# A two-layer network after linear attention: seven-product multiplication of the second product taken one level further from the third strip on

## The chip, the cores and the metric

The kernel runs on one NeuronCore of a Trainium2 chip. The time is the device time in microseconds of one execution. Everything is fp32. TensorE (PE) multiplies from SBUF into PSUM banks; VectorE (DVE) and ScalarE (ACT) read PSUM and SBUF; GpSimd (POOL) works in SBUF; SyncE (SP) issues the transfers. Each engine runs its instructions in the order in which they were written.

## What is computed

```python
# q, k, v: (8, 8, 576, 64); w_in: (512, 2048); w_out: (2048, 512), given as 64-bit floats
kv = np.einsum('bhsd,bhse->bhde', k, v)
out = np.einsum('bhsd,bhde->bhse', q, kv)
rms = np.sqrt(np.mean(out * out, axis=-1, keepdims=True) + 1e-06)
x = (out / rms * g_norm)                 # then (B, H, S, D) -> (4608, 512)
h = x @ w_in
r = np.maximum(h, 0.0)
y = (r * r) @ w_out                      # (4608, 512)
```

## The kernel before

The 4608 rows of x are 36 tiles of 128, worked off in nine strips of four tiles (512 rows). A strip has a first product, x @ w_in with the squared ReLU, and a second one with w_out. While a strip is multiplied, the attention work for the next one is done in small slices between the steps.

**Products.** Apart from strip 0's first product (`up_first`, L579, 512-column matmuls), each product is one level of a seven-product scheme of Strassen's kind: the operands are cut in halves both ways, seven products of halves with prepared sums are formed instead of eight, and the results are put together. `up` (L597) does it for each of four groups g of the 2048 hidden features: seven products p in `ORDER` (L536), each of 2 x 2 matmuls with 256 columns. `down` (L631) does it for the second product: seven products, each two steps i of eight matmuls with 256 columns. `product` (L548) issues them all, on L551. The banks are A (two of them), B and C: `open_bank` (L542) opens one for p = 1, 5, 2, later products accumulate into them. `combine` (L556) takes the results out: ACT copies `snap` of p = 1, 6, 5, and one addition for each of 2, 7, 3, on DVE; p = 4 is copied by ACT.

**Operand sums.** The hidden quarters 11, 12, 21, 22 and a fifth tile 1 for a sum are `gt` tiles of 128 x 2048 from `g_pool` (five). `sums_g` (L575) makes two differences or sums per group in the first product; `down` makes two more over whole quarters (L643, L645). `sums_x` (L469) makes four sums of x, as a slice, when the strip's four tiles are there. w_in lies in SBUF with its sums (`sums_in`, L235). w_out's seven blocks lie in DRAM (`w_out`, L164) and are streamed, 1 MB per product, into three slots (`stream`, L625): each is asked for when a product has ended.

**Attention slices** (L479 to L511): `transposed_query` and `key_value` for each pair of heads of a batch, then per tile `query` (products, root mean square, scaling) and, from the third batch on, `squares_x`, which turns the tile by way of DRAM, and `scale_x` (L459), which multiplies by g_norm on ACT. `attend` at L699 spreads a strip's slices over 85% of its steps' weight. `key_value` asks for the next pair's k, v, q (`load_next`) into three slots each; the store of the output, eight transfers for one `o_sb` tile, is issued on SP too (L656), as are all loads.

**Strip 0** also converts w_in and w_out from 64-bit floats: `convert_on_act` on ACT, `conversion` on DVE, `sums_out` (L246) for w_out's sums. The `raw` slots of this work are given back at L688, and the pools opened there take their place.

## Time and profile before

| | |
|---|---|
| median of 3 runs | 987.95 us (987.73 to 988.01) |
| profiled execution | 989.48 us, of it 987.7 us span from the first to the last instruction |
| mean granted TensorE clock | 0.994 |
| strip 0's first product begins | 38.6 us |
| strip 0's second product begins | 101.6 us |
| strip 1's first product begins | 158.5 us |
| last strip's second product | 932.5 to 980.7 us |
| DMA | 139.79 MB, mean 142 GB/s |

The span is what the trace covers; the execution's own time has a little around it. An engine's busy share is an average over stages with different limits. Matmuls are pipelined: the duration in a row (379 ns for 256 columns) is longer than the distance from one to the next. A source-level fp32 matmul shows as two instructions.

### The profile page before, as it was taken

To read this page: it belongs to the slowest core of one execution; us is meant where nothing else is said; L and a number is where in the kernel's file an instruction comes from. 1 tells how busy PE (TensorE), PEld (TensorE's weight loads), DVE (VectorE), ACT (ScalarE), POOL (GpSimd) and SP (SyncE) were. 2 spreads that over 40 slices of the span, in tenths; PEclk is the share of its full clock that TensorE was granted. 3 is DMA by queue.
4 is the path that set the end of the run, shared out by engine and by line. 5 is a ranking of instruction groups with operands and counts; after the bars stand their busy time and mean duration, and the time that the engine had idled before them with its cause. 6 is when DMAs were issued, how large, how long until landed. Compare 5 with 4: busy or idle time off the path is not lost.

```text
span 987.7 us, 12864 instructions
## 1 busy us (share of the span) xinstructions
PE 956.9 (97%) x4968; PEld 810.8 (82%) x4968; DVE 457.3 (46%) x826; ACT 244.7 (25%) x510; POOL 1.7 (0%) x7
## 2 busy tenths in 40 slices
PE   3799999999999999999999999999999999999997
PEld 3444888888888888888888888888888888888886
DVE  3899872463255424462356335343545155214320
ACT  3698311221122102211222122111321022002200
POOL 0000000000000000000000000000000000000000
PEclk9799999999999999999999999999999999999999
DMA  8689775425633463446344642475114610450041
GB/s 251 214 268 322 259 213 194 96 70 192 213 74 88 160 199 103 94 135 204 111 97 114 201 149 62 125 188 186 43 33 155 207 43 22 160 193 10 1 155 58
DMA packets 150108, 139.79 MB, mean 142 GB/s; under 512 B 84128, under 2 KB 130720, under 8 KB 142368
## 3 DMA queue, kind: packets, MB, share of 16 engines
q1 hardware_dynamic: 149888, 138.98, 46.2%
q8 instruction: 39, 0.64, 0.3%
q14 instruction: 21, 0.17, 0.1%
q10 hardware_dynamic: 160, 0.00, 0.0%
HBM read 115.08 MB, written 23.86 MB: 141 GB/s over the span
## 4 chain that ended last, share of the span: by engine, by line
PE 88%; DVE 6%; DMA 2%; ACT 2%; issue 1%; SPq 1%; DVEq 0%; ACTq 0%
PE ps_A L551 47%; PE ps_B L551 24%; PE ps_C L551 12%; PE x_ps L362 2%; PE kv_ps L333 2%; DVE w_c L208 1%; DVE wt L228 1%; DMA raw<-in_moe_w_out_dram 1%; DVE w_c L202 1%; DMA raw<-in_moe_w_in_dram 1%; DVE w_in L211 1%; DMA q_rest<-in_q_dram 1%; ACT w_c L190 0%; ACT raw L193 0%; DVE wt L211 0%
## 5 line engine op out<-in xcount | busy, mean ns | idle before, releaser
L551 PE MATMUL ps_A<-w_blk,gt 128*128 128x256 f32 x1120 | 249.0, 379 | 0.7 <-ACT snap L561 0.7
L551 PEld LDWEIGHTS ps_A<-w_blk,gt 128*128 128x128 f32 x1120 | 211.7, 190 | 29.6 <-ACT snap L561 1.1
L551 PE MATMUL ps_A<-x_t,w_in 128*128 128x256 f32 x768 | 182.6, 381 | 0.7 <-DVE gt L610 0.7
L551 PEld LDWEIGHTS ps_A<-x_t,w_in 128*128 128x128 f32 x768 | 144.8, 190 | 20.9 <-DVE gt L610 1.1
L551 PE MATMUL ps_B<-w_blk,gt 128*128 128x256 f32 x544 | 121.0, 379 | 0.0
L551 PEld LDWEIGHTS ps_B<-w_blk,gt 128*128 128x128 f32 x544 | 103.0, 190 | 13.8
L561 ACT COPY snap<-ps_A 128x512 f32<-128x512 f32 x82 | 47.9, 585 | 187.2 <-PE ps_A L551 187.2
L228 DVE TENSOR_TENSOR gt<-gt 128x512 f32<-128x512 f32 (+1 forms) x54 | 66.2, 1225 | 41.9 <-PE ps_A L551 23.1
L610 DVE TENSOR_TENSOR gt<-ps_C,snap 128x512 f32<-128x512 f32 x32 | 22.1, 692 | 128.3 <-PE ps_C L551 128.3
L610 DVE TENSOR_TENSOR gt<-ps_A,snap 128x512 f32<-128x512 f32 x32 | 22.1, 692 | 102.5 <-PE ps_A L551 102.3
L611 DVE SCALAR_TENSOR_TENSOR gt<-gt 128x512 f32<-128x512 f32 x96 | 66.5, 692 | 3.3
L551 PE MATMUL ps_A<-xT,w_in 128*128 128x256 f32 x256 | 61.0, 381 | 0.0
L551 PE MATMUL ps_B<-xT,w_in 128*128 128x256 f32 x256 | 61.0, 381 | 0.0
L551 PE MATMUL ps_C<-xT,w_in 128*128 128x256 f32 x256 | 60.6, 379 | 0.0
L551 PE MATMUL ps_B<-x_t,w_in 128*128 128x256 f32 x256 | 60.5, 379 | 0.0
L370 DVE TENSOR_REDUCE ms<-sq 128x8 f32<-128x512 f32 x36 | 24.6, 684 | 75.2 <-ACT sq L368 75.1
L551 PE MATMUL ps_C<-w_blk,gt 128*128 128x256 f32 x256 | 57.5, 380 | 0.0
L551 PEld LDWEIGHTS ps_C<-xT,w_in 128*128 128x128 f32 x256 | 48.6, 190 | 6.7 <-issue 0.2
L551 PEld LDWEIGHTS ps_A<-xT,w_in 128*128 128x128 f32 x256 | 48.2, 190 | 6.7
L551 PEld LDWEIGHTS ps_B<-xT,w_in 128*128 128x128 f32 x256 | 48.2, 190 | 6.6
L551 PEld LDWEIGHTS ps_B<-x_t,w_in 128*128 128x128 f32 x256 | 48.3, 190 | 6.4
L551 PEld LDWEIGHTS ps_C<-w_blk,gt 128*128 128x128 f32 x256 | 48.2, 190 | 6.6 <-issue 0.2
(90 smaller groups left out, 769.1 us busy)
## 6 DMA issues: line engine op xcount, KB each, us to landing
w_blk<-w_out SPq DMA_DIRECT2D x60, 1024.0 KB, 5.1
k<-in_k_dram SPq DMA_DIRECT2D x32, 256.0 KB, 3.1
v<-in_v_dram SPq DMA_DIRECT2D x32, 256.0 KB, 3.4
raw<-in_moe_w_in_dram SPq DMA_DIRECT2D x16, 512.0 KB, 6.4
raw<-in_moe_w_out_dram SPq DMA_DIRECT2D x16, 512.0 KB, 5.2
x_d<-x_q SPq DMA_DIRECT2D x27, 256.0 KB, 2.4
xT<-x_d SPq DMA_DIRECT2D x108, 64.0 KB, 2.0
q<-in_q_dram SPq DMA_DIRECT2D x96, 64.0 KB, 3.1
```

The lines of the kernel that those rows point to most:

```text
L202: yield nc.vector.tensor_scalar(out=c, in0=c, scalar1=LEAST, scalar2=MOST, op0=ALU.max, op1=ALU.min)
L208: yield nc.vector.scalar_tensor_tensor(out=ci, in0=high, scalar=-(2**30), in1=ci, op0=ALU.bitwise_and, op1=ALU.bitwise_or)
L211: yield nc.vector.tensor_tensor(out=dest.bitcast(I32), in0=ci, in1=r, op=ALU.add)
L228: eng.tensor_tensor(out=out, in0=a, in1=b, op=ALU.subtract)
L333: nc.tensor.matmul(ps[ts(h, D)], lhsT=a, rhs=w, start=c == 0, stop=c == C)
L362: nc.tensor.matmul(o, lhsT=qT[b, p][:, c_b, :], rhs=kvd[b, p], start=True, stop=True)
L370: nc.vector.reduce_sum(out=ms, in_=by_head(sq), axis=AX.X)
L551: nc.tensor.matmul(bank[BANK[p]][:, i, :], lhsT=lhsT(k), rhs=rhs(k), start=p in (1, 5, 2) and i == 0 and k == 0, stop=k == n - 1, skip_gro ...
L561: nc.scalar.copy(snap[p], b)
L610: nc.vector.tensor_tensor(out=o, in0=b, in1=a, op=ALU.add)
L611: nc.vector.scalar_tensor_tensor(out=o, in0=o, scalar=0.0, in1=o, op0=ALU.max, op1=ALU.mult)
```

## The change

Strips 0 and 1 (`DEEP = 2`) keep their second product. From strip 2 on each of its seven products is cut once more by the same scheme: 49 small products, each four matmuls with 128 columns. A level-1 product is two steps: the leaves 1, 2 and 4, whose left operands are plain blocks of a quarter, then 5, 6, 7 and 3, whose left operands are sums that `leaf_sums` makes on DVE one product ahead. Each level-1 product uses two PSUM banks, turn about on A+A and C+B; `together` takes the previous product's result out, with a copy on ACT and four additions on DVE, and adds the finished partial results into the output tiles. The sums over whole quarters (formerly `sums_g` and two differences) are made in the first and third product, two of them on GpSimd. The order of the seven is 4, 1, 2, 6, 5, 7, 3.

The right operands need W_out's sums of the second level: strip 1 makes them on DVE (`deep_sums`) and writes them to DRAM (`w_deep`). From strip 2 on a level-1 product streams two tiles, three blocks (0.75 MB) from `w_out` and four (1 MB) from `w_deep`, into four slots; `stream(2)` is called at a product's end, for the product after the next. `w_out` is laid out in column blocks of 128 for this and written in pieces of 512 bytes.

Along with it: g_norm is multiplied into w_in once (`sums_in`) instead of into x (`scale_x` is gone; strip 0's x keeps it); attention is spread over 42% of a strip's weight instead of 85%; `sums_x` is called at fixed steps; `g_pool` has four tiles instead of five, the fifth quarter being four small tiles (`g_s1`) in strips 0 and 1; strip 0's `sums_g` are all made at the start of its second product; q, k and v have two slots instead of three, pairs 2 and 3 of the first batch lie in `g_pool` slots, and two `load_next` calls of strip 0 are gone, one being added in `key_value`; `snap`, `o_sb` and the partial results share six slots (`c_pool`), the sums of x and of the quarters eight (`sum_pool`).

```diff
...
+    DEEP = 2
...
-    qkv_pool = ctx.enter_context(tc.tile_pool(name="qkv", bufs=3))
+    qkv_pool = ctx.enter_context(tc.tile_pool(name="qkv", bufs=2))
...
-    g_pool = ctx.enter_context(tc.tile_pool(name="g", bufs=5))
+    g_pool = ctx.enter_context(tc.tile_pool(name="g", bufs=4))
...
-    osb_pool = ctx.enter_context(tc.tile_pool(name="osb", bufs=2))
...
-    w_out = dram.tile([7, P, FQ, DH], FP32, name="w_out")
+    w_out = dram.tile([7, P, 2, FQ, P], FP32, name="w_out")
+    w_deep = dram.tile([7, P, 4, FQ // 2, P], FP32, name="w_deep")
...
     def sums_in(g):
+        nc.scalar.activation(w_in[:, :, g, 0:4], w_in[:, :, g, 0:4], AF.Copy, scale=g_col)
...
-            nc.sync.dma_start(out=w_out[3:7, :, j, :].rearrange("b p e -> p b e"), in_=x)
+            for e in range(2):
+                nc.sync.dma_start(out=w_out[3:7, :, e, j].rearrange("b p e -> p b e"), in_=x[:, :, ts(e, P)])
...
         if b < 2:
-            if b == 1 and p == 0:
+            if b == 1 and p < 2:
...
-        nc.scalar.activation(
-            x[:, ts(i, 4)].rearrange("p a q t -> p q a t"), ps.rearrange("p q (a t) -> p q a t", a=4),
-            AF.Copy, scale=g_col,
-        )
+        nc.scalar.copy(x[:, ts(i, 4)].rearrange("p a q t -> p q a t"), ps.rearrange("p q (a t) -> p q a t", a=4))
...
-    def scale_x(n):
-        s, i = divmod(n, NT)
-        o = xt[s][:, ts(i, 4)]
-        nc.scalar.activation(o, o, AF.Copy, scale=g_col)
...
-            xc_pool.tile([P, TH // SQ, KH, SQ], FP32, name=f"x_t{i}", tag=f"x_t{i}") for i in range(4)
+            sum_pool.tile([P, TH // SQ, KH, SQ], FP32, name=f"x_t{i}", tag="sum") for i in range(4)
...
-        for i in range(len(ns) + 2):
+        for i in range(len(ns) + 1):
...
-            done = ns[i - 1] if b < X_ON_PE and 0 < i <= len(ns) else ns[i - 2] if b >= X_ON_PE and i > 1 else None
-            if done is not None:
-                if b >= X_ON_PE:
-                    slices.append((scale_x, (done,)))
-                if done % NT == NT - 1:
-                    if done // NT:
-                        slices.append((sums_x, (done // NT,)))
-                    ready[done // NT] = len(slices)
+            if i > 0 and ns[i - 1] % NT == NT - 1:
+                ready[ns[i - 1] // NT] = len(slices)
...
    def quarters(s, g):
-        if (s, 1) not in gq:
-            for q in (11, 12, 21, 22, 1):
+        if (s, 11) not in gq:
+            for q in (11, 12, 21, 22):
...
-        return {q: gq[s, q][:, 2 * g : 2 * g + 2, :] for q in (11, 12, 21, 22, 1)}
-    def sums_g(dest):
-        nc.vector.tensor_tensor(out=dest[1], in0=dest[12], in1=dest[22], op=ALU.add)
+        return {q: gq[s, q][:, 2 * g : 2 * g + 2, :] for q in (11, 12, 21, 22)}
+    def sums_g(s, g):
+        dest = quarters(s, g)
+        s1 = gq[s, 1, g] = sum_pool.tile([P, 2, TH], FP32, name="g_s1", tag="sum")
+        nc.vector.tensor_tensor(out=s1, in0=dest[12], in1=dest[22], op=ALU.add)
...
-        if g > 0 and fh == 1 and i == 0:
-            sums_g(quarters(0, g - 1))
...
-                if q == 12:
-                    sums_g(dest)
+                if q == 12 and s < DEEP:
+                    sums_g(s, g)
...
-    w_blk[0, 1], w_blk[0, 2], w_blk[0, 5] = w_first
-    to_stream = iter([(s, p) for s in range(N_STRIP) for p in ORDER if (s, p) not in w_blk])
-    def stream():
-        u = next(to_stream, None)
-        if u is not None:
-            w_blk[u] = stream_pool.tile([P, FQ, DH], FP32, name="w_blk", tag="w_blk")
-            nc.sync.dma_start(out=w_blk[u], in_=w_out[B_OUT[u[1]]])
+    for p, t in zip((1, 2, 5), w_first):
+        w_blk[0, p] = t.rearrange("p f (h e) -> p h f e", h=2)
+    DEEP_ORDER = (4, 1, 2, 6, 5, 7, 3)
+    to_stream = [(s, p) for s in range(DEEP) for p in ORDER if (s, p) not in w_blk]
+    to_stream += [(s, p, n) for s in range(DEEP, N_STRIP) for p in DEEP_ORDER for n in range(2)]
+    to_stream = iter(to_stream)
+    def stream(n=1):
+        for _, u in zip(range(n), to_stream):
+            s, p = u[:2]
+            t = stream_pool.tile([P, 4, FQ // 2, P], FP32, name="w_blk", tag="w_blk")
+            if s < DEEP:
+                w_blk[u] = t.rearrange("p (h a) f e -> p h (a f) e", h=2)
+                nc.sync.dma_start(out=w_blk[u], in_=w_out[B_OUT[p]])
+            elif u[2] == 0:
+                nc.sync.dma_start(
+                    out=t[:, 1:4], in_=w_out[B_OUT[p]].rearrange("p h (a f) e -> p (h a) f e", a=2)[:, 1:4]
+                )
+                w_blk[s, p, 3], w_blk[s, p, 1], w_blk[s, p, 2] = (t[:, i] for i in range(1, 4))
+            else:
+                nc.sync.dma_start(out=t, in_=w_deep[B_OUT[p]])
+                w_blk[s, p, 5], w_blk[s, p, 6], w_blk[s, p, 7], w_blk[s, p, 4] = (t[:, i] for i in range(4))
+    def out_tile():
+        return c_pool.tile([P, 2, DH], FP32, name="o_sb", tag="c")
+    def send(s, th, eh, o):
+        for t in range(2):
+            for part, rows in out_rows(NT * s + 2 * th + t):
+                nc.sync.dma_start(out=rows[:, ts(eh, DH)], in_=o[part, t, :])
...
-        a = gq[s, {1: 11, 2: 21, 6: 11, 5: 1, 7: 12, 3: 21, 4: 22}[p]]
+        a = {1: 11, 2: 21, 6: 11, 7: 12, 3: 21, 4: 22}.get(p)
...
-        product(p, i, lambda fc: a[:, fc, ts(i, P)], lambda fc: w[:, fc, :], FQ)
+        product(
+            p, i,
+            lambda fc: (gq[s, 1, fc // 2][:, fc % 2] if p == 5 else gq[s, a][:, fc])[:, ts(i, P)],
+            lambda fc: w[:, :, fc], FQ,
+        )
         if i == 0:
+            if s == DEEP - 1:
+                deep_sums(p, w)
...
-        if s > 0 or p not in (1, 2, 5):
+        if s == 0 and p in (6, 7, 3) or s == DEEP - 1 and p not in (3, 4):
...
+        if s == DEEP - 1:
+            nc.sync.dma_start(out=w_deep[B_OUT[p]], in_=deep.pop(p))
         if p == 1:
-            minus(nc.vector, gq[s, 11], gq[s, 1], gq[s, 11])
+            for g in range(NG):
+                x = gq[s, 11][:, ts(g, 2)]
+                minus(nc.vector, x, gq[s, 1, g], x)
...
             def f(b, a=None):
-                o = osb_pool.tile([P, 2, DH], FP32, name="o_sb", tag="o_sb")
+                o = out_tile()
...
-                for t in range(2):
-                    for part, rows in out_rows(NT * s + 2 * th + t):
-                        nc.sync.dma_start(out=rows[:, ts(eh, DH)], in_=o[part, t, :])
+                send(s, th, eh, o)
...
+    deep = {}
+    def deep_sums(p, w):
+        t = deep[p] = stream_pool.tile([P, 4, FQ // 2, P], FP32, name="w_t", tag="w_blk")
+        b11, b12, b21, b22 = (w[:, e, ts(f, FQ // 2)] for f in range(2) for e in (1, 0))
+        minus(nc.vector, t[:, 0], b12, b11)
+        minus(nc.vector, t[:, 1], b22, t[:, 0])
+        minus(nc.vector, t[:, 2], b22, b12)
+        minus(nc.vector, t[:, 3], b21, t[:, 1])
+    A_G = {4: 22, 1: 11, 2: 21, 6: 11, 5: 22, 7: 12, 3: 21}
+    leaf, chain, part = {}, {}, {}
+    def leaf_sums(s, p):
+        a = gq[s, A_G[p]]
+        a11, a12, a21, a22 = (a[:, ts(f, FQ // 2), ts(t, P)] for t in range(2) for f in range(2))
+        s1, s2, s3, s4 = (sum_pool.tile([P, FQ // 2, P], FP32, name=f"g_s{i}", tag="sum") for i in range(4))
+        leaf[p] = {1: a11, 2: a12, 3: s4, 4: a22, 5: s1, 6: s2, 7: s3}
+        nc.vector.tensor_tensor(out=s1, in0=a21, in1=a22, op=ALU.add)
+        minus(nc.vector, s2, s1, a11)
+        minus(nc.vector, s3, a11, a21)
+        minus(nc.vector, s4, a12, s2)
+    PLACE = {1: (0, 0), 2: (0, 1), 6: (0, 2), 5: (1, 0), 7: (1, 1), 3: (1, 2), 4: (1, 3)}
+    def small_products(s, p, js):
+        c = "B" if p in (4, 2, 5, 3) else "A"
+        if js[0] == 1 and p not in (6, 7, 3):
+            chain[c] = [
+                fpsum.tile([P, 4, P], FP32, name=f"ps_{c}", tag=t, bufs=2 if t == "A" else 1)
+                for t in ("AA" if c == "A" else "CB")
+            ]
+        for j in js:
+            x, i = PLACE[j]
+            a, w = leaf[p][j], w_blk.pop((s, p, j))
+            for f in range(FQ // 2):
+                nc.tensor.matmul(
+                    chain[c][x][:, i, :], lhsT=a[:, f, :], rhs=w[:, f, :],
+                    start=p not in (6, 7, 3) and j in (1, 4) and f == 0, stop=f == FQ // 2 - 1, skip_group_check=True,
+                )
+    def together(p):
+        x, y = chain["B" if p in (4, 2, 5, 3) else "A"]
+        o = part[p] = out_tile()
+        q = o.rearrange("p t (h e) -> p (t h) e", h=2)
+        one = lambda t: t.to_broadcast([P, 2, P])
+        add = lambda out, a, b: nc.vector.tensor_tensor(out=out, in0=a, in1=b, op=ALU.add)
+        nc.scalar.copy(q[:, 3], x[:, 0])
+        add(q[:, 1:3], one(q[:, 3:4]), x[:, 1:3])
+        add(q[:, 0:4:3], one(q[:, 2:3]), y[:, 0:2])
+        add(q[:, 2], q[:, 3], y[:, 0])
+        add(q[:, 0:4:3], q[:, 0:4:3], y[:, 2:4])
+        for a, th, eh in {2: [(1, 0, 0)], 7: [(4, 1, 0), (5, 1, 1)], 3: [(6, 0, 1)]}.get(p, []):
+            add(part[a], part[a], o)
+            send(s, th, eh, part[a])
+    def down_deep(s, k, js):
+        p = DEEP_ORDER[k]
+        small_products(s, p, js)
+        before = DEEP_ORDER[k - 1] if k else None
+        after = DEEP_ORDER[k + 1] if k < 6 else None
+        g = lambda q: gq[s, q]
+        if js[0] == 1:
+            if k:
+                together(before)
+            if k == 0:
+                leaf_sums(s, after)
+                nc.vector.tensor_tensor(out=g(22), in0=g(12), in1=g(22), op=ALU.add)
+                minus(nc.gpsimd, g(12), g(11), g(12))
+            if k == 2:
+                minus(nc.vector, g(11), g(22), g(11))
+                minus(nc.gpsimd, g(21), g(21), g(11))
+            if 0 < k < 6:
+                leaf_sums(s, after)
+            if k == 6 and s + 1 < N_STRIP:
+                sums_x(s + 1)
+        else:
+            stream(2)
+            if k == 6:
+                together(p)
...
-        steps += [(2, down, (s, p, i)) for p in (ORDER if s else (1, 2, 5, 6, 7, 3, 4)) for i in range(2)]
+        if s < DEEP:
+            steps += [(2, down, (s, p, i)) for p in (ORDER if s else (1, 2, 5, 6, 7, 3, 4)) for i in range(2)]
+        else:
+            steps += [(2, down_deep, (s, k, js)) for k in range(7) for js in ((1, 2, 4), (5, 6, 7, 3))]
...
-                if i in (2, 4, 6):
+                if i in (2, 4):
...
-                xc_pool = ctx.enter_context(tc.tile_pool(name="xc", bufs=1, reuse_waits="tile"))
-                snap_pool = ctx.enter_context(tc.tile_pool(name="snap", bufs=1, reuse_waits="tile"))
-                stream_pool = ctx.enter_context(tc.tile_pool(name="stream", bufs=3, reuse_waits="tile"))
-                for _ in range(3):
-                    stream()
+                sum_pool = ctx.enter_context(tc.tile_pool(name="sum", bufs=8, reuse_waits="tile"))
+                c_pool = ctx.enter_context(tc.tile_pool(name="c", bufs=6, reuse_waits="tile"))
+                stream_pool = ctx.enter_context(tc.tile_pool(name="stream", bufs=4, reuse_waits="tile"))
+                stream(3)
+                for g in range(NG):
+                    sums_g(0, g)
...
-                    nc.sync.dma_start(out=w_out[b], in_=t)
+                    for e in range(2):
+                        nc.sync.dma_start(out=w_out[b, :, e], in_=t[:, :, ts(e, P)])
...
             if s:
-                attend(ready[s] + int((goal - ready[s]) * min(done / (0.85 * total), 1)))
+                attend(ready[s] + int((goal - ready[s]) * min(done / (0.42 * total), 1)))
+                if s >= DEEP and i == n_up - 3:
+                    leaf_sums(s, 4)
+                if s == DEEP - 1 and i == len(steps) - 1:
+                    sums_x(s + 1)
+                    stream(4)
...
-            if i == n_up:
-                sums_g(quarters(0, NG - 1))
...
             if i == n_up + 6:
-                load_next()
...
-                for g in range(NG):
-                    sums_in(g)
+            if i - n_up in (6, 8, 10, 12):
+                sums_in((i - n_up - 6) // 2)
+            if i == n_up + 9:
+                sums_x(1)
...
```

## Prediction

> **What bounds the kernel now.** I read the page first: busy shares and the chain of waits. Then the busy time by stage, the groups by shape, the timeline around one attention product, and the DMA issues.
>
> ```profile
> span 987.7 us, 12864 instructions
> ...
> PE 956.9 (97%) x4968; PEld 810.8 (82%) x4968; DVE 457.3 (46%) x826; ACT 244.7 (25%) x510; POOL 1.7 (0%) x7
> ...
> PE 88%; DVE 6%; DMA 2%; ACT 2%; issue 1%; SPq 1%; DVEq 0%; ACTq 0%
> ```
>
> TensorE (PE) is busy nearly throughout and is 88% of the chain. Where it is not the bound shows by stage (stretch, length, then busy time and instructions of PE, weight load, DVE, ACT, POOL, clock, DMA share, GB/s):
>
> ```profile
> 38.60:101.60 63.00, 63.00 (x230) 29.42 (x229) 61.22 (x137) 56.58 (x129) 0.00 (x0) 0.96 0.88 275
> 101.60:158.50 56.90, 55.59 (x291) 48.61 (x289) 37.52 (x76) 9.42 (x22) 0.00 (x0) 1.00 0.80 258
> 158.50:213.80 55.30, 54.61 (x326) 47.01 (x326) 27.18 (x48) 14.90 (x32) 0.00 (x0) 1.00 0.36 89
> 836.00:884.00 48.00, 48.00 (x225) 42.24 (x224) 10.85 (x12) 4.84 (x8) 0.00 (x0) 1.00 0.46 159
> ```
>
> The first two are strip 0's first and second product, the third strip 1's first, the last strip 7's second. From strip 1 on PE has no gap worth the name; strip 7's second product is 224 instructions in 48 us with DVE idle three quarters of the time. So PE instructions taken out there come off the span one for one, until DVE, a bank or a stream is late. Only strip 0 is also tight on DVE (61.2 of 63.0).
>
> The price of a PE instruction is its pace, not its duration, since they are pipelined:
>
> ```profile
> 480.02 1.89 PE L551 MATMUL ps_A<-x_t,w_in 128*128 128x256 f32 x8
> 640.53 1.08 PEld L362 LDWEIGHTS x_ps<-kv_all,qT 128*128 128x128 f32 x8
> 640.74 1.05 PE L362 MATMUL x_ps<-kv_all,qT 128*128 128x128 f32 x8
> 648.21 5.30 SPq L656 DMA_DIRECT2D out_dram<-o_sb  x8
> ```
>
> With 256 columns: eight in 1.89, the last lasting 0.379 (its group's mean), so (1.89-0.379)/7 = 0.216 us each. With 128 columns and a new stationary tile for every product, as the change has it: (1.05-0.275)/7 = 0.111 us. Half the columns cost 51%, so small products are nearly free of a penalty.
>
> **PE, the term that carries the change.** Each fp32 product of the source is two instructions in the trace (a strip's second product is 7 x 2 x 8 = 112 products, 224 records). Before, per strip: 224 x 0.216 = 48.4 us. After: 49 products of 4 chunks, two instructions each, 392 x 0.111 = 43.5 us. That is 4.9 us a strip, and strips 2 to 8 are seven: **-34 us**. The bounds on the pace: 0.108 (half of 0.216; 392 x 0.108 = 42.3, -42 us in all) and 0.127, the weight loads' own row, (1.08-0.192)/7, if those set it over a long run; that is 49.8, +10 us in all. I take 0.111, since the 0.127 contains the long gap after the first load, which was pulled under a 256-column product. Break-even is 48.4/392 = 0.123.
>
> **DVE, per strip from 2 on.** Durations:
>
> ```profile
> L228 DVE TENSOR_TENSOR gt<-gt 128x2048 f32<-128x2048 f32 x18 | 41.3, 2292 | 40.7 <-PE ps_A L551 23.1 <-PE ps_C L551 17.5
> L576 DVE TENSOR_TENSOR gt<-gt 128x512 f32<-128x512 f32 x36 | 24.9, 691 | 1.1
> L228 DVE TENSOR_TENSOR wt<-wt 128x256 f32<-128x256 f32 x8 | 3.0, 417 | 0.0
> L324 ACT COPY qT_rest<-tr_ps 128x128 f32<-128x128 f32 x4 | 1.1, 269 | 0.0
> L274 POOL MEMSET kv_all<- 128x1152 f32 x1 | 1.1, 1058 | 0.0
> masks.py:199 POOL TENSOR_SCALAR_AFFINE_SELECT ident<-ident 128x128 f32<-128x128 f32 x1 | 0.3, 294 | 0.1
> ```
>
> Added: leaf_sums 7 x 4 x 0.69 = 19.3; together 7 x (3 x 0.417 + about 0.28 for 128 columns, between the 0.17 of the eight-wide rows and 0.417) = 10.7; four closing additions 2.8; two whole quarter sums 4.6: 37.4 us in a stage of 43.5. Removed: sums_g 8 x 0.69 = 5.5, the two 2048-wide differences 4.6, three output additions 2.1; ACT gives up four 0.59 copies for seven of 0.27. DVE fits, but at 86%, and in order. One level-1 product lasts 24 x 0.111 = 2.7 (leaves 1, 2, 4, which need no sums) plus 32 x 0.111 = 3.6 (5, 6, 7, 3), 6.2 us. Behind it on DVE, in order: together for the product before (0.45 for the last matmul's semaphore and ACT's copy, 1.5 for the adds), then the four sums for the product after. Those are due 6.2 + 2.7 = 8.9 us after the step begins, and banks read by together are needed only one product later, so 5 to 7 us of DVE work lie under PE. The tightest step is the third, with a 2.29 sum besides: 0.45 + 1.5 + 2.3 + 2.8 = 7.1.
>
> **POOL.** Two 2048-wide differences a strip, a form the trace does not hold. By the memset's rate 1.06/1152 x 2048 = 1.9 us, by the affine select's 16 x 0.294 = 4.7 us; I take 4.7, since that one reads SBUF too. Their results are first read 14 us later or more, so their length is hidden; what counts is whether DVE stops meanwhile. The Trainium skill (SBUF — State Buffer, Who interferes with whom) says that it does: DVE with two SBUF inputs and a GpSimd instruction that reads SBUF exclude each other for a whole instruction. No row here shows the two together; by that rule the sum is that of the second rival below, without it that of the forecast.
>
> **The W_out stream.** Per strip 7 x (0.75 + 1) = 12.25 MB instead of 7, in four slots: a pair is asked for when product k ends and is due at k+2: the first tile after 6.2 us, the second, whose first use is leaf 4, after 8.0.
>
> ```profile
> w_blk<-w_out SPq DMA_DIRECT2D x60, 1024.0 KB, 5.1
> ...
> w_blk<-w_out SPq DMA_DIRECT2D x3, 1024.0 KB, 7.0
> ...
> DMA to landing us min/median/max: 4.7/5.1/10.3
> ```
>
> The x3 row is three loads issued back to back at 110.35: the second landed some 7.0 us after its issue at 110.8, 7.4 after the first's. A pair a quarter smaller lands at about 6.8 against 8.0, so it is hidden with 1.2 us to spare. What it is queued behind on SP: the eight output stores that follow the third product's closing addition, 3.4 us at 0.42 each and 5.3 with a load in flight (L656 above). They end 6.5 to 8.5 us into a step whose end, at 6.2, should issue the next pair: 0 to 2.3 late, less the 1.2 spare. With DVE jitter I put all stalls of the deep stage at 1 us a strip, **+7** (bounds 0, and 3.3 x 7 = 23 from the second rival).
>
> **Attention drawn into 42% of a strip's steps.** Same PE work, denser in the first product. The densest stage now (158.5 to 213.8) loses 0.7 us, strip 0's second product 1.3. Loads of q, k, v look two units ahead instead of three: three slices of some 3 us each (0.42 x 56 steps of about 1.95 us for some 15 slices), 9 us, against 3.4 us of issue on SP plus 3.1 of landing. Seven stages at 0 to 1.3: **+3.5**. scale_x, 27 x 0.719 on ACT, goes; its cover was PE, so it brings nothing.
>
> **Strips 0 and 1.** Moved: sums_g out of strip 0's first product (three groups, 4.1 us of a DVE that is busy 61.2 of 63.0) to the head of its second, all eight at once (5.5 us), into slots that the last converted pieces leave; one q/k/v load later; W_out written in 512-byte pieces (16 + 6 stores instead of 8 + 3); four ACT scalings of w_in, 2048 wide, some 2 us each by the 0.59 us per 512, under PE; sums_x later, before it is due. DVE already held PE up at 111.5 for 0.64 us; if the eight sums must wait for stores that end near 111 (last issue 106.7, median landing 4.0), they end at 116.5, not 108.8: +8. If all fits, the relieved DVE gives up to 3: -3. I take **+1**. Strip 1's deep_sums (19.3 us DVE) and 7 MB written to w_deep lie in a stage with 37 us of DVE idle.
>
> **End.** Now 981.1 to 987.7. After: ACT 0.3, adds 1.5 and 0.7, then eight stores that queue on SP behind sixteen from the seventh product: about **+2** (0 to 4).
>
> **Sum.** -34 + 7 + 3.5 + 1 + 2 = -20.5. The profiled execution took 989.48 us (span 987.7 and 1.8 around it), so 969.0; the median of the three runs is 987.95, 1.5 less. Forecast for the median: 987.95 - 20.5 = **967.5**, its own range 960 to 978.
>
> **Rivals.** *Nothing stalls* (chance 0.12): -34 to -42 with strip 0 at -3: 950 to 955. For: spare in every window above. Against: DVE at 86% in order.
>
> *POOL and DVE exclude each other* (0.2): in the third step POOL's 4.7 us fall in front of three of the four sums; they end 24 us into the stage instead of 19.5, the closing addition and its eight stores start 4.5 later, at 26.5, the pair for the sixth product is issued at 30 instead of 25 and lands 1.7 and 0.8 late, after 0.8 at a bank: 3.3 us a strip, 23 in all. 967.5 + 16 = 984 (980 to 990). For: two-input DVE work stands on both sides. Against: no row with both engines at work.
>
> *The stream becomes the bound*, the other side (0.1): the place is products 3 to 7, where each pair is asked for only when its slots come free. From a landing of 8.0 each us costs 5 x 7 = 35; the forecast's 20 are spent at 8.6. For: a 1 MB load took 10.3 once, and the stage needs 12.8e6 bytes/43.5 us = 295 GB/s where the page's best slice has 322. Against: the x3 row. At 9.2 us: +42 instead of some +5, 1005.
>
> The weight loads setting 0.127 (0.03) would give 1011.
>
> **Chances.** Forecast 0.55, rivals 0.12, 0.2, 0.1, 0.03. A change of 0.2% (2 us) is what this measurement can tell. Faster: 0.55 + 0.12 + half of the POOL case, 0.77; same 0.07; slower 0.16. Range 952 to 990: it leaves out the last two cases and the far end of the first rival.
>
> **What would show it.** Eight small products in 0.89 us on PE; a deep second product of 43.5 to 45 us with DVE near 37; no PE idle behind w_blk; DVE two-input instructions beside POOL at 0.69. A PE wait on w_blk, leaf sums lasting 5 us, or a pace above 0.123 would make it wrong.

## The result, and the profile after

The changed kernel takes 1012.09 us (median of 4 runs, 1007.17 to 1014.63), the one before 987.84 (987.23 to 988.01): 1.0241 of it, 95% interval 1.0201 to 1.0280. It is slower by 2.4%, where 2% faster was forecast. The profiled execution is the shortest of the four, 1007.17 us with a span of 1005.4; the others took 4.3 to 7.5 us more, at a mean granted clock of 0.977 to 0.979 against its 0.983. They were not traced, so what follows explains the 17.7 us between the spans 987.7 and 1005.4.

From the page of the changed kernel: the span, the busy shares, the chain of waits by engine, and the POOL group:

```profile
span 1005.4 us, 15784 instructions
...
PE 937.5 (93%) x6144; PEld 828.0 (82%) x6144; DVE 684.7 (68%) x1203; ACT 230.5 (23%) x508; POOL 67.9 (7%) x21
...
PE 66%; DVE 23%; DMA 6%; issue 2%; ACT 2%; SPq 1%; DVEq 0%
...
L241 POOL TENSOR_TENSOR gt<-gt 128x2048 f32<-128x2048 f32 x14 | 66.2, 4726 | 902.0 <-DVE gt L764 856.6
```

PE's busy time fell by 19.4 us as wished, yet PE is 66% of the chain instead of 88%: DVE now stands on it with 23% and DMA with 6%. The POOL subtraction lasts 4.73 us on average.

By stage (stretch, length, busy time and instructions of PE, weight load, DVE, ACT, POOL, then clock, DMA share, GB/s): strip 0's second product, then the deep second products of strips 2, 5 and 8:

```profile
101.30:163.30 62.00, 56.98 (x291) 49.79 (x290) 37.92 (x77) 16.96 (x27) 0.00 (x0) 0.97 0.70 215
324.40:372.40 48.00, 44.55 (x394) 44.01 (x394) 42.51 (x62) 3.09 (x9) 9.44 (x2) 1.00 0.65 238
638.00:688.60 50.60, 45.86 (x393) 45.51 (x392) 42.44 (x62) 3.08 (x9) 9.45 (x2) 0.97 0.63 228
...
947.40:996.20 48.80, 44.41 (x392) 43.87 (x392) 40.12 (x58) 3.09 (x9) 9.45 (x2) 1.00 0.56 199
```

The deep stages were to last 43.5 us plus 1. From the first matmul of each to the first of the next stage (the table's bounds are rounded) they last 48.0, 48.6, 49.6, 50.7, 50.1, 51.6 and 48.8, in sum 347.4 us, about what 256-column products took (48.4 each, 339). So the whole gain of 34 us is given back inside these stages, and in places the clock goes down as well. Strip 0's second product is 5.1 us longer than before (56.9). What PE waited for, over the whole span (in total, times, longest):

```profile
PE ps_A L731 <- DMA w_blk<-w_out: 20.1, 7, 3.6
...
PE ps_A L731 <- DVE g_s L241: 8.3, 8, 1.2
...
PE xt_ps L453 <- DVE x_n L405: 4.3, 1, 4.3
...
PE ps_A L731 <- DMA w_blk<-w_deep: 1.1, 2, 0.6
```

In each of the seven stages the first W_out tile of a pair (the two tiles of one level-1 product) is late once, and one sum is late, in the last stage two. Where they come from is in the timeline of strip 2 from its third product on (start, duration, engine, line; in brackets the idle time before and what ended it):

```profile
342.53 4.93 POOL L241 TENSOR_TENSOR gt<-gt 128x2048 f32<-128x2048 f32 x1 [6.48 <-PE ps_B L731]
343.12 4.89 DVE L241 TENSOR_TENSOR g_s<-g_s,gt 128x512 f32<-128x512 f32 x1
...
348.06 2.94 PE L731 MATMUL ps_A<-w_blk,g_s 128*128 128x128 f32 x24 [1.13 <-DVE g_s L241]
...
350.88 0.69 DVE L742 TENSOR_TENSOR o_sb<-o_sb 128x512 f32<-128x512 f32 x1
...
351.60 2.22 SPq L653 DMA_DIRECT2D out_dram<-o_sb  x5
...
353.91 0.37 SPq L639 DMA_DIRECT2D w_blk<-w_out  x1
...
354.38 0.55 SPq L644 DMA_DIRECT2D w_blk<-w_deep  x1
...
359.09 2.02 PE L731 MATMUL ps_A<-w_blk,gt 128*128 128x128 f32 x16 [1.83 <-DMA w_blk<-w_out]
...
361.60 0.57 PE L731 MATMUL ps_A<-w_blk,gt 128*128 128x128 f32 x3 [0.48 <-DMA w_blk<-w_deep]
```

Read it downwards. POOL begins its subtraction; a DVE sum of 512 elements, 0.69 us where POOL is idle, is held until POOL is done and lasts 4.89. The sums behind it are late, PE waits 1.13 us. The closing addition comes at 350.88, and SP, which works in order, has its stores (351.60) ahead of the next pair of W_out tiles. The slots of that pair were free when product 6, the fourth, ended, by 351.0 (348.06 + 2.94); it is issued at 353.91 and 354.38. PE, which needs it 1.83 us before it is there, stops.

In later strips that wait is longer, 2.4 to 3.6 us, because the pair goes out later: five stores stand ahead of it in strip 2, six in strip 3, eight from strip 4 on. It is issued 3.0 us after the closing addition begins in strip 2, 3.8 in strip 3 and 4.4 to 5.3 after that. Strip 5:

```profile
664.39 0.69 DVE L742 TENSOR_TENSOR o_sb<-o_sb 128x512 f32<-128x512 f32 x1
...
665.12 4.51 SPq L653 DMA_DIRECT2D out_dram<-o_sb  x8
...
669.72 0.37 SPq L639 DMA_DIRECT2D w_blk<-w_out  x1
```

From strip 4 to strip 7 the clock goes down there too. Strip 4, the same place, in the timeline:

```profile
568.11 4.54 PE L731 MATMUL ps_A<-w_blk,gt 128*128 128x128 f32 x24 [2.59 <-DMA w_blk<-w_out]
```

and the stretch behind it (columns as in the table by stage):

```profile
568.50:572.00 3.50, 3.50 (x19) 3.50 (x18) 2.14 (x4) 0.00 (x0) 0.00 (x0) 0.51 0.99 375
```

Twenty-four small matmul instructions take 4.54 us instead of 2.84: PE runs at a granted clock of 0.5 for 3.4 us. The deep stages of strips 4 to 7 hold 17.1 us of this in all.

### The profile page after: what moved, and what is told of

The parts are those of the page before. It is cut to its first block, busy times and chain, and to the rows that moved or that the text cites. A ratio compares the mean times of both kernels' runs of the same rounds, so it can differ in the third digit from the quotient of the medians.

```text
span 1005.4 us, 15784 instructions
## 1 busy us (share of the span) xinstructions
PE 937.5 (93%) x6144; PEld 828.0 (82%) x6144; DVE 684.7 (68%) x1203; ACT 230.5 (23%) x508; POOL 67.9 (7%) x21
## 4 chain that ended last, share of the span: by engine, by line
PE 66%; DVE 23%; DMA 6%; issue 2%; ACT 2%; SPq 1%; DVEq 0%
PE ps_A L552 25%; PE ps_B L552 12%; DVE g_s L241 8%; PE ps_C L552 7%; PE ps_B L731 7%; PE ps_A L731 6%; DVE g_s L712 4%; DVE o_sb L742 3%; PE ps_A L588 2%; PE x_ps L378 2%; DMA w_blk<-w_out 2%; PE kv_ps L349 2%; DVE gt L241 2%; DVE gt L764 2%; DMA w_blk<-w_deep 1%
## 5 line engine op out<-in xcount | busy, mean ns | idle before, releaser
L241 POOL TENSOR_TENSOR gt<-gt 128x2048 f32<-128x2048 f32 x14 | 66.2, 4726 | 902.0 <-DVE gt L764 856.6
L731 PE MATMUL ps_B<-w_blk,g_s 128*128 128x128 f32 x896 | 104.6, 275 | 0.0
L731 PEld LDWEIGHTS ps_B<-w_blk,g_s 128*128 128x128 f32 x896 | 102.3, 192 | 0.0
L731 PE MATMUL ps_A<-w_blk,gt 128*128 128x128 f32 x504 | 68.2, 297 | 21.6 <-DMA w_blk<-w_out 20.1
L731 PE MATMUL ps_A<-w_blk,g_s 128*128 128x128 f32 x672 | 80.5, 276 | 7.9 <-DVE g_s L241 7.9
L731 PEld LDWEIGHTS ps_A<-w_blk,g_s 128*128 128x128 f32 x672 | 77.5, 192 | 9.2 <-DVE g_s L241 9.2
L731 PEld LDWEIGHTS ps_A<-w_blk,gt 128*128 128x128 f32 x504 | 65.3, 211 | 23.2 <-issue 21.2
L731 PE MATMUL ps_B<-w_blk,gt 128*128 128x128 f32 x672 | 79.6, 275 | 0.0
L241 DVE TENSOR_TENSOR g_s<-g_s,gt 128x512 f32<-128x512 f32 x49 | 63.3, 1291 | 1.7
L712 DVE TENSOR_TENSOR g_s<-gt 128x512 f32<-128x512 f32 x49 | 54.5, 1112 | 0.5
```

Source lines behind the costliest of these rows:

```text
L241: eng.tensor_tensor(out=out, in0=a, in1=b, op=ALU.subtract)
L712: nc.vector.tensor_tensor(out=s1, in0=a21, in1=a22, op=ALU.add)
L731: nc.tensor.matmul(chain[c][x][:, i, :], lhsT=a[:, f, :], rhs=w[:, f, :], start=p not in (6, 7, 3) and j in (1, 4) and f == 0, stop=f == F ...
```

## Experiments

Each kernel below differs from the changed one only by what its diff shows. Spans and stages are from one profiled execution of each; the sum of the seven deep stages is the figure to watch: 347.4 us as changed. Executions of one kernel of the deeper scheme differ by 3 to 8 us, so single spans a few us apart decide nothing; the one kernel that was traced twice has 314.1 for this sum both times.

**Without the POOL subtractions.**

```diff
-                minus(nc.gpsimd, g(12), g(11), g(12))
...
-                minus(nc.gpsimd, g(21), g(21), g(11))
```

> Leaves out the two 2048-wide differences on POOL in each deep stage (strips 2 to 8), so products 7 and 3 read activations that were not subtracted; all other work, the W_out stream and the stores stay. Theory (a POOL subtraction and DVE's two-input sums from SBUF hold each other up, and the late closing addition and its stores then make SP issue the next W_out pair late): every 512-wide sum on DVE at 0.69, no 4.9; the seven deep stages 44 to 45.5 us each instead of a mean of 49.6, so the span falls from 1005.4 by some 30 to 40 to 965 to 975, and the half-clock stretches in the deep stages go. Rival 1 (the stream is the bound: a pair lands too late by itself): PE still waits for w_blk 2 us or more in each deep stage, 47 to 48 us each, span 995 or more. Rival 2 (DVE is the bound, 37 us of short work in order within 43.5): the stages give back only the 4.9 - 0.7 of one sum each, 46 to 48 us, span 985 to 1000.

Measured: span 977.6 us, deep stages 44.1, 44.8, 44.7, 44.4, 48.1, 46.1, 44.9, in sum 317.1: 30.3 us less than with POOL. The groups by shape:

```profile
L241 DVE TENSOR_TENSOR g_s<-g_s,gt 128x512 f32<-128x512 f32 x49 | 33.9, 692 | 1.7
L712 DVE TENSOR_TENSOR g_s<-gt 128x512 f32<-128x512 f32 x49 | 33.6, 686 | 0.5
```

and the waits for W_out tiles in the deep stages:

```profile
PE ps_A L731 <- DMA w_blk<-w_deep: 3.3, 4, 1.9
...
PE ps_A L731 <- DMA w_blk<-w_out: 0.5, 2, 0.3
```

The same two groups took 63.3 and 54.5 us in the changed kernel (means 1291 and 1112 ns): POOL's 66 us of work held DVE for 50 us, 7.2 a strip. PE's waits for W_out tiles in these stages fell from 21.2 to 3.8, though every byte of the stream was still loaded, so the stream was not what bound the changed kernel. Strip 6 kept one wait of 1.9 us and one stretch at half clock; the span missed its expected 965 to 975 by that and by strip 0, whose second product took 63.6 us here.

**The subtractions on DVE.**

```diff
-                minus(nc.gpsimd, g(12), g(11), g(12))
+                minus(nc.vector, g(12), g(11), g(12))
...
-                minus(nc.gpsimd, g(21), g(21), g(11))
+                minus(nc.vector, g(21), g(21), g(11))
```

> The two 2048-wide differences go from POOL to DVE, nothing else. Theory: no POOL beside DVE, every sum at its own price (0.69, 2.29), DVE 42 of 43.5 us and in order; in the third step the sums for product 6 come 2 x 2.29 after the copy and adds, about as late as the POOL wait made them, in the first step the sums for product 2 come late by less than 1; deep stages 45 to 48 us, span 975 to 995: part of the loss comes back, not all. Rival 2 (DVE's load and order are the bound whoever does the difference): as slow as the changed kernel or slower, 49 to 51 us, span 1003 to 1015. Rival 1 (stream): PE's waits for w_blk as before, 48 to 50 us, span about 1000.

Span 986.6 us, deep stages 44.9 to 48.1, sum 326.8. Two thirds of what leaving them out gained comes back although DVE now does all the work itself, 2 x 2.29 us a strip more. DVE's load is therefore not what made the changed kernel slow. It still costs something in this order: PE's waits on late pairs are 8.7 and 2.8 us.

**The pairs ahead of the stores on SP.** POOL keeps its work.

```diff
-            send(s, th, eh, part[a])
+            late.append((s, th, eh, part[a]))
...
             stream(2)
+            while late:
+                send(*late.pop(0))
             if k == 6:
                 together(p)
+            while late:
+                send(*late.pop(0))
```

> POOL's differences stay; on SP, in each step the pair of W_out tiles is asked for before the output stores of that step, not behind them. Theory: DVE's 4.9 us sums and PE's waits for g_s (8.3 us over the seven stages) stay, but PE's waits for w_blk (20.1 us over the seven) fall below 6 since a pair no longer queues behind stores that wait for a late addition, and most half-clock stretches in the deep stages go with them: stages 45 to 47 us, span 978 to 992. Rival 1 (landing time or the slots make pairs late, not the queue): waits for w_blk stay at 15 to 20 us, span 1000 to 1008. Rival 2 (DVE's lateness is everything, pairs only follow): waits move from w_blk to g_s, stages 48 or more.

Span 985.2 us, sum 323.5, and no stretch at half clock in any deep stage. The timeline of strip 2, at the place shown above:

```profile
346.62 4.89 DVE L241 TENSOR_TENSOR g_s<-g_s,gt 128x512 f32<-128x512 f32 x1
...
351.56 2.94 PE L732 MATMUL ps_A<-w_blk,g_s 128*128 128x128 f32 x24 [1.14 <-DVE g_s L241]
353.65 0.32 SPq L639 DMA_DIRECT2D w_blk<-w_out  x1
...
354.54 0.32 SPq L644 DMA_DIRECT2D w_blk<-w_deep  x1
355.10 2.85 SPq L653 DMA_DIRECT2D out_dram<-o_sb  x5
```

and of the waits over the span:

```profile
PE ps_A L732 <- DVE g_s L241: 7.7, 7, 1.1
...
PE ps_B L732 <- DMA w_blk<-w_deep: 1.6, 4, 0.5
...
PE ps_B L732 <- DMA w_blk<-w_out: 1.4, 4, 0.6
```

The hold of 4.89 is still there and PE still waits 1.14 for the sum, 7.7 us over the seven strips. But the pair goes out when the product ends, the stores after it, and PE's waits for W_out tiles are 3.2 us instead of 21.2 (the rows, and 0.2 on the other banks). So of the loss in the deep stages 24 us needed both: a late addition and stores queued ahead of the pair. Taking away either one removes it, which is why the gains of this kernel and of the one without POOL (23.9 and 30.3) do not add.

**Strip 0's sums one step later.**

```diff
                 stream(3)
-                for g in range(NG):
-                    sums_g(0, g)
...
+            if s == 0 and i == n_up + 1:
+                for g in range(NG):
+                    sums_g(0, g)
             fn(*a)
```

> Strip 0 alone: its eight sums of activations come one step of the second product later, behind the next strip's attention work on DVE instead of ahead of it. Theory (they wait 3.49 us for the stores of the converted W_out pieces, whose bytes their tiles take, and hold up the attention work behind them, for which PE then waits and is clocked down): strip 0's second product falls from 62.0 us to 57 to 59, no half-clock stretch near 115 us, the span from 1005.4 to 1000 to 1002.5, deep stages as they were. Rival (strip 0's DVE is simply behind, 61 us of work before): the wait moves to product 5 or to a bank, second product 61 to 63 us, span unchanged within 1.5.

In the changed kernel's timeline the first of these sums waits for the stores on whose bytes its tile lies, and the next strip's attention work behind it on DVE makes PE wait:

```profile
108.09 0.69 DVE L579 TENSOR_TENSOR g_s<-gt 128x512 f32<-128x512 f32 x1 [3.49 <-DMA w_out<-wt]
...
114.90 1.11 PE L453 MATMUL xt_ps<-ident,x_n 128*128 128x128 f32 x4 [4.34 <-DVE x_n L405]
```

With the sums behind that work, the stage is 57.4 us long, against 62.0 as changed, 63.6 to 64.0 in the three kernels above and 56.9 before the change:

```profile
100.20:157.60 57.40, 55.50 (x293) 48.51 (x290) 38.44 (x79) 17.68 (x30) 0.00 (x0) 1.00 0.77 236
```

The span fell only to 1003.2, above the expected 1000 to 1002.5: the deep stages took 349.2 here and strip 1's second product 1.6 us more, in single waits that are not in the same places in the two traces.

**The POOL work in four pieces.** If POOL and DVE share a path by the element, small pieces change nothing in kind; if one holds the other for a whole instruction, the hold becomes as long as a piece.

```diff
-                minus(nc.gpsimd, g(12), g(11), g(12))
+                for f in range(NG):
+                    minus(nc.gpsimd, g(12)[:, ts(f, 2)], g(11)[:, ts(f, 2)], g(12)[:, ts(f, 2)])
...
-                minus(nc.gpsimd, g(21), g(21), g(11))
+                for f in range(NG):
+                    minus(nc.gpsimd, g(21)[:, ts(f, 2)], g(21)[:, ts(f, 2)], g(11)[:, ts(f, 2)])
```

> The changed kernel with each 2048-wide POOL subtraction in four of 512; the same work in all. If DVE and POOL hold each other up for one whole instruction at a time: no DVE sum lasts 4.9 any more, but two to four sums each wait for a piece of 1.2 (1.2 to 2 us each), the sums end about as late, deep stages 48 to 51, span 1000 to 1008. If POOL merely slows DVE by sharing (no exclusion): sums of 1 to 1.5 as long as POOL is at work, the same sum of time. If only the one long hold did the harm: deep stages 45 to 47, span 980 to 990.

Span 1005.6 us, deep stages 47.4 to 51.6, sum 344.4: no better. The timeline of strip 2's third step:

```profile
345.75 6.72 POOL L241 TENSOR_TENSOR gt<-gt 128x512 f32<-128x512 f32 x4 [5.16 <-PE ps_B L731]
346.34 1.64 DVE L241 TENSOR_TENSOR g_s<-g_s,gt 128x512 f32<-128x512 f32 x1
347.90 1.75 DVE L241 TENSOR_TENSOR g_s<-gt 128x512 f32<-128x512 f32 x1
349.58 1.75 DVE L241 TENSOR_TENSOR g_s<-gt,g_s 128x512 f32<-128x512 f32 x1
351.26 1.71 DVE L742 TENSOR_TENSOR o_sb<-o_sb,ps_B 128x256 f32<-128x256 f32 x4
```

The two engines take turns. Each DVE sum waits for one piece (1.64 to 1.75 instead of 0.69), POOL waits for DVE in between (four pieces in 6.72 us against 4.93 in one), and the additions that read PSUM run beside POOL at their usual 0.42 each. Over the span the 196 sums take 177.0 us, against 184.8 in the changed kernel and 134.5 without POOL: the holds are shorter, but their sum is nearly the same, and so is the time.

**The repairs together.** No POOL work at all: with g12 replaced by g11 - g12 group by group in the first product, where DVE has time, the later sums are g22 - g12, g11 + g22 and g21 - g22, placed on DVE behind the four sums that are due first. The two repairs above come with it.

```diff
                 if q == 12 and s < DEEP:
                     sums_g(s, g)
+                elif q == 12:
+                    minus(nc.vector, o, dest[11], o)
...
-    A_G = {4: 22, 1: 11, 2: 21, 6: 11, 5: 22, 7: 12, 3: 21}
+    A_G = {4: 22, 1: 11, 2: 21, 6: 22, 5: 11, 7: 12, 3: 21}
...
+            if k < 6:
+                leaf_sums(s, after)
             if k == 0:
-                leaf_sums(s, after)
-                nc.vector.tensor_tensor(out=g(22), in0=g(12), in1=g(22), op=ALU.add)
-                minus(nc.gpsimd, g(12), g(11), g(12))
+                minus(nc.vector, g(22), g(22), g(12))
             if k == 2:
-                minus(nc.vector, g(11), g(22), g(11))
-                minus(nc.gpsimd, g(21), g(21), g(11))
-            if 0 < k < 6:
-                leaf_sums(s, after)
+                nc.vector.tensor_tensor(out=g(11), in0=g(11), in1=g(22), op=ALU.add)
+            if k == 4:
+                minus(nc.vector, g(21), g(21), g(22))
```

> The whole computation, three edits: no work on POOL (the difference g11 - g12 is taken group by group in the first product, then g22 - g12, g11 + g22 and g21 - g22 on DVE in the steps for products 4, 2 and 6, always behind the four sums that are due first); the next pair asked for ahead of the stores; strip 0's sums one step later. Theory: deep stages 43.8 to 45 us (sum 307 to 315 instead of 347.4), strip 0's second product 57 to 58.5, no half-clock stretch after 105 us but at the very end, span 960 to 969, time 962 to 971, ratio to the kernel before 0.975 to 0.983. Rival 2 (DVE's load is the bound: 40 us of 43.5): deep stages 46 to 48 and span 975 to 990. Rival 1 (stream): PE waits for w_blk of 2 us and more in each deep stage, span 975 or more.

972.12 us (median of 5, 969.96 to 972.91) against 988.22 before: 0.9835, interval 0.9821 to 0.9848. The profiled span is 968.2, the deep stages sum to 314.0. By stage, strips 2, 5 and 8:

```profile
320.30:364.20 43.90, 43.90 (x393) 43.81 (x392) 38.23 (x64) 3.09 (x9) 0.00 (x0) 1.00 0.72 259
622.10:668.00 45.90, 44.44 (x394) 44.00 (x393) 38.31 (x64) 3.09 (x9) 0.00 (x0) 1.00 0.69 253
...
915.30:960.10 44.80, 44.16 (x392) 43.81 (x392) 35.85 (x60) 3.08 (x9) 0.00 (x0) 1.00 0.62 219
```

PE is busy without a gap in strip 2 with DVE at 38.2 of 43.9, 87%, and the clock stays at 1.00. The sum of the stages is as expected, though three of them lie above 45 us (45.1, 45.9, 45.7); the median is a microsecond above what was expected. The remaining waits in the deep stages are 3.4 us for W_out tiles and 0.8 for output sums.

**The same with the stores ahead of the pairs again**, in a single execution and then in several.

> The last one with the stores again ahead of the next pair on SP, as the change has it. Theory: with no late addition the stores end in time in most steps; some waits for w_blk of 0 to 2 us stay in single strips, as where the POOL work was left out: deep stages 44 to 46.5, sum 310 to 320, span 962 to 974. If the order on SP is a cause by itself, without POOL: sum above 325, span above 978.

> The kernel without POOL work, stores ahead of the pair, timed in rounds. If the order on SP matters only where an addition is late, which is so only beside POOL: 968 to 972 us, within 2 of the version that asks for the pairs first (972.1). If it matters by itself: 975 or more.

The single execution: span 967.4 us, deep sum 314.1 us. Then 972.45 us (median of 4, 971.73 to 976.9), 0.9855, interval 0.9835 to 0.9875. The median is half a microsecond above what was expected and can't be told from that of the version above; the trace of one of these four has a deep sum of 314.1 again. Where no addition is late, SP's order costs nothing that these runs can show.

**POOL kept, with the two other repairs.** The edits are those of the third and fourth experiments.

> The changed kernel with POOL's differences kept, the pairs asked for first and strip 0's sums later. If the two repairs add (1005.4 - 20.2 from the pairs; strip 0's second product 57.4 instead of 64.0 there): span 977 to 981, deep stages 45 to 47 with one PE wait of 1.1 on g_s each. If they overlap: 982 to 986.

Span 976.3 us, deep sum 323.2, strip 0's second product 57.4: the two repairs add, slightly better than expected, with one stage (48.1) above the expected 45 to 47. PE waits 6.6 us for late sums in seven waits. What POOL itself still costs here is the 9.2 us of the deep stages between this kernel and the one without it.

**More stream.** On the kernel with the repairs together the first tile of each pair is loaded whole.

```diff
-                    out=t[:, 1:4], in_=w_out[B_OUT[p]].rearrange("p h (a f) e -> p (h a) f e", a=2)[:, 1:4]
+                    out=t, in_=w_out[B_OUT[p]].rearrange("p h (a f) e -> p (h a) f e", a=2)
```

> The first of these kernels with the first tile of each pair loaded whole, 1 MB instead of 0.75 (14 MB a strip instead of 12.25; the fourth part is loaded and not used). Theory (the stream has about 1 us to spare): a pair lands 0.5 to 1.2 us later, PE's waits for w_blk come to 0 to 2 us a strip, deep stages 44.5 to 46.5, span 962 to 980. Rival 1 (the stream is at its limit, rate-bound): 1.75 MB more a strip at 295 GB/s cost 5 to 6 us a strip, deep stages 49 or more, span 1000.

Span 972.5, deep sum 321.0: 1.0 us a strip for 1.75 MB more, a fifth to a sixth of what a stream at its limit would cost by the expectation. Two stages (47.7, 47.4) lie above the expected 46.5. PE's waits for these tiles are 7.5 us instead of 3.4. The stream is hidden, but with little left over.

**The last stores on two queues.** On the kernel with the stores ahead of the pairs.

```diff
+                eng = nc.scalar if tail and t else nc.sync
-                nc.sync.dma_start(out=rows[:, ts(eh, DH)], in_=o[part, t, :])
+                eng.dma_start(out=rows[:, ts(eh, DH)], in_=o[part, t, :])
...
-            send(s, th, eh, part[a])
+            send(s, th, eh, part[a], s == N_STRIP - 1 and p in (7, 3))
```

> The kernel without POOL work, with the stores ahead of the pair and strip 0's sums later, and in the last strip half of the 24 stores after the seventh and third products issued on ACT's queue. Theory (24 stores in a row on SP, 11 us, end some 3.6 us after the last addition): the time from PE's end to the span's end falls from about 8.8 to 6.5 or 7, so 1.5 to 2.5 us less than the same kernel with all stores on SP: 966 to 969.5. Rival (the last store's landing or ACT's copy behind the waiting stores sets the end): no difference, or up to 1 us more.

The end of the span with all stores on SP (a trace of that kernel), then with two queues:

```profile
956.75 11.01 SPq L655 DMA_DIRECT2D out_dram<-o_sb  x24
...
962.28 0.69 DVE L744 TENSOR_TENSOR o_sb<-o_sb 128x512 f32<-128x512 f32 x1
```

```profile
952.05 8.27 SPq L656 DMA_DIRECT2D out_dram<-o_sb  x12
952.10 3.68 ACTq L656 DMA_DIRECT2D out_dram<-o_sb  x8
...
957.88 0.69 DVE L745 TENSOR_TENSOR o_sb<-o_sb 128x512 f32<-128x512 f32 x1
958.60 1.79 ACTq L656 DMA_DIRECT2D out_dram<-o_sb  x4
```

On one queue the issue of the 24 stores ends 4.8 us after the last addition (962.97 to 967.76), on two 1.8 (958.57 to 960.39). PE ended at 961.0 and 956.3, the spans at 969.9 and 962.8: 8.9 us are left after PE with one queue, 6.5 with two. Time 970.84 us (median of 5, 964.56 to 972.53), 0.9808, interval 0.9781 to 0.9835, above the expected 966 to 969.5. The traces show 2.4 us; the medians differ by 1.6 with overlapping intervals, so the time alone doesn't show it. This is the lowest of the medians, 1.9% below the kernel before, though its interval overlaps those of the two versions above.

## Why the prediction was wrong

Its terms against the profiled executions:

| term | forecast, us | measured, us |
|---|---|---|
| small products on PE | -34 | -33 (43.7 us in the freest deep stages instead of 48.4) |
| stalls in the deep stages | +7 | +42.9 (347.4 less 7 x 43.5; 41.5 by 43.7) |
| attention packed into 42% | +3.5 | about +1.5 (what the other rows leave) |
| strips 0 and 1 | +1 | +5.1 in strip 0's second product |
| end | +2 | +2.2 |

With -34 and 43.5 the measured column makes +17.7, the difference of the spans; the attention row was not measured by itself.

**Right:** the pace. Twenty-four small matmul instructions take 2.84 us, the last lasting 0.275: (2.84 - 0.275)/23 = 0.1115 against 0.111. Freed of its stalls the change brings what the forecast said of it: the kernel with the repairs has a span 19.5 us below that before, where the forecast's sum was -20.5.

**The step that failed** is the sentence "With DVE jitter I put all stalls of the deep stage at 1 us a strip, +7". These stalls came to 42.9 us. The step took each DVE sum at 0.69 also beside POOL (the section on POOL had left open which of two sums holds), so it had the closing addition, and with it the stores and the pair behind them, 4.5 us earlier than the rival below, which was right on this. The rival "POOL and DVE exclude each other" had the mechanism, at 0.2, and most of its steps came out to the half microsecond in strip 2: the closing addition 26.5 us into the stage (measured 26.5: 350.88 - 324.40), the pair issued at 30 (29.5), late by 1.7 and 0.8 (1.83 and 0.48). The 0.8 us at a bank that it also counted did not come: no deep stage of the changed kernel has a PE wait of that kind. The rule that speaks for it, in the Trainium skill (SBUF — State Buffer, Who interferes with whom), holds here: two-input sums of DVE from SBUF wait for a whole POOL instruction that reads SBUF (4.89 instead of 0.69), those with one input in PSUM do not (0.42). It was given too little weight for want of a row showing both engines; the changed kernel's trace has that row (343.12).

**The rival was itself too cheap**, 3.3 us a strip against 6.1. Of the 42.9 us, PE's waits for W_out tiles are 21.2 and those for sums 8.3. The second kind it did not price at all: it said that the sums end at 24 us, and not that PE needs the second of them at 22.5 (346.93). Half-clock stretches are 17.1 us long; PE was idle for 1.6 of them and lost about half of the rest, 7.7. It had nothing on the clock. Of the 5.7 that remain, 1.4 are the 0.2 a strip between 43.5 and 43.7, and some 2.8 belong to the 17 waits: idle time counts from the end of the last matmul, 0.275 after its start, where the next would have started after 0.111. The rest was not followed up. The wait for the late tile also grew after strip 2, to between 3.2 and 3.6 in strips 5 to 7: the rival had the pair issued at 30 with eight stores ahead of it; strip 2, with five, has 29.5, and strips 4 to 8, with eight, have 30.8 to 31.8. Why the eight take 4.5 us to issue in strips 5 and 7 and 3.6 in strip 4 is open.

**The other side.** "The stream becomes the bound" forecast a slower kernel through PE's waits on w_blk, and these are the largest of PE's waits in the deep stages, 20.1 us. Yet its mechanism fell: the tile issued at 353.91 was there 5.2 us later, within the forecast's 6.8, only it was issued 3 us late; without POOL, and with POOL but the pair issued first, the same stream left 3.8 and 3.2 us. The row names what came last, not what was late first.

**Strip 0** went well towards its upper bound, 5.1 of 8, by the mechanism given for the +8: the sums wait for the last stores (3.49 us). The value of +1 was chosen between -3 and +8 although DVE was known to be behind there. One step later in the program brings the stage to 57.4.

**What would have made it wrong** was named rightly: a PE wait on w_blk and leaf sums lasting 5 us, and both came. The first rival's 950 to 955 does not follow from its own terms: -34 to -42 with no stalls and strip 0 at -3, attention and end as forecast, makes 948 to 956.

## What to carry to other kernels

Work moved to an engine that looks free is not free if, as here, its instructions hold up those of the busy one: count how often the busy one would be held, and for how long, before trusting that a result is not needed for 14 us. On an in-order queue, issue first what the critical engine waits for and then what waits for a late result: a store that waits for its data delays every load behind it. On DVE 38.2 us of work in a stage of 43.9 was fine where every piece stood in the order of its due time; 35.3 us of its own work (42.5 less 7.2 of holds) with one late piece was not.

## What the runs showed of the hardware

- Stretches at a granted clock of 0.5 start on a grid of 3.413 us: in the changed kernel they begin 0, 23, 156, 187, 218, 248 and 282 periods after the first (36.12 us; the third at 568.60, 532.48/156 = 3.413), and all but the last, which is at the span's end, last one or two. Over the traces of these kernels, in the deep stages, no wait of PE up to 1.83 us was followed by one, every wait from 3.38 us was, and between 1.92 and 3.22 some were and some not (1.92 was, 3.22 in one trace was not). The Trainium skill (TensorE: Matmul & The Clock Gate, HAM oscillation — how this bites in real kernels) gives idle gaps above some 3.4 us as the limit; here such a stretch came with six waits of 1.92 to 2.90 us.
- POOL's subtraction of 2048 elements took 4.52 us where its first DVE neighbour read PSUM, and 4.93 where it began behind a two-input DVE sum already under way.
- The kernels with the deeper scheme spread by 3 to 8 us between executions of one kernel, the one before by under 2.
